# Scaled float16 parts in all three pair passes of an attention and mixture-of-experts kernel

## The chip, the core and the metric

The kernel runs as one program on one core of a Trainium2 chip. The metric is the device time of one execution in microseconds. Three runs of the kernel before took 1152.30, 1151.19 and 1151.82 us; their median, 1151.82 us, is the time that the change is measured against.

## The reference, cut to what matters

```
x   = attention(q, k, v)                 # (4, 8, 768, 64): 3072 tokens of 512
p   = domain_probs / (sum over experts + 1e-9)
out = 0
for e in range(4):
    h    = maximum(x @ w1[e], 0)         # 512 -> 1024
    out += p[:, e] * (h @ w2[e])         # 1024 -> 512
```

Attention is a local window of 16 keys to either side, together with one summary key (a maximum) and one summary value (a mean) of each block of 32 keys, under one softmax. All inputs and outputs are float32, and every expert sees every token, so the matmuls of the four experts are most of the work.

## The kernel before, in words

**Precision.** TensorE is not fed plain float32. A value is split into a high and a low part, and each product is three matmuls: high by high, high by low, low by high. There are two kinds of parts. The wide kind is float32r. The narrow kind is float16; its operands are first multiplied by a power of two taken from the largest absolute value of the operand, and the powers are divided out in the mixing weights (`mixed`, L1006).

**Tokens and passes.** The 3072 tokens are eight blocks of 384 (`TB`). The two blocks of one batch form a pair, and `plan` (L1405) lists six passes: block 0 with experts 0 and 1, block 1 with experts 1 and 0, blocks 0 and 1 with experts 2 and 3, and then pair 1, pair 2 and pair 3 with all four experts each. The first three are the plain passes. A pair pass does its first layer by Strassen's seven products (`SEVEN`, L1157) on halves of tokens, rows and columns: 4 quarters `i` of an expert, 7 products, 6 matmuls of 384 columns each. The second layer of pairs 1 and 2 is plain (`second`, L1083): 6 token tiles, 8 chunks of rows, 3 matmuls of 512 columns. Pair 3 uses seven products there too.

**Which parts where.** `SCALED = NTB // 2 - 2` (L185) is 2: pairs 2 and 3 use float16 parts, the plain passes and pair 1 float32r.

**Weights.** In the plain passes and in pair 1, `weights` (L783) and `w1_operands` (L804) load raw float32 rows and split them with ScalarE (the high part) and GpSimd or VectorE (the low part). `split_weights` (L768) also writes every expert's split w2 to a DRAM tile (`stored`); pair 1 reads it back. For float16, `prepare` (L875) is a generator with 32 jobs, two rows of w1 or w2 each: it loads the rows, makes the scaled parts on ScalarE and VectorE, with the sums for w1 on GpSimd, and writes the parts to DRAM for pair 3. Steps of it are taken at fixed units: `LATE` (11 steps in the last expert of the pass before), and `FIRST` and `SECOND` (10 steps each in every expert's first and second layer). So 4 jobs run ahead of the pass and 28 in it. `fetch_last` (L951) reads the w1 parts back for pair 3.

**Finding the powers.** The largest w1 and w2 values of expert 2 are scanned by VectorE reductions in the plain pass (`scan_plain`, `scan_w2`), those of the other three experts in pair 1 (`scan_w1`, `scan_w2`). `scan_v` (L366) does the same for v of batches 2 and 3, one reduction in each attention piece, and bounds x. `spread_maxima` (L143) then passes a maximum over the partitions by a write to DRAM and a broadcast read, 6 and 8 us of planned matmul time apart.

**Order.** Attention is cut into pieces of 96 queries by 4 heads, 16 in a batch; `ENDS` (L37) says at which piece each pass stops, and `advance` interleaves them with the matmuls in proportion to the work done. Pairs 1 and 2 thus carry pieces of the batches that come next. A piece's probabilities are turned by a DMA transpose (`transposed`, tile awT), and TensorE waits for it before the product with v (tile px). All DMAs are issued in order by one queue, SyncE's. The program is written in priority order, and a scheduler places each engine's instructions after that order and its own estimate of times.

Two buffer pools matter: `x` (14 tiles of 3 KB, for x operands; float32r operands of a pair take all 14, float16 operands 7) and `w2` (8 tiles of 4 KB).

Of the kernel before, what the change touches and what calls it, by code (L numbers as in the profile page):

```python
# [12 lines left out]
I32 = mybir.dt.int32  # L13
# [53 lines left out]
def attn_moe(ctx: ExitStack, tc: tile.TileContext, qvL, qv0, v0L, kD, kT, vT, w1L, w2L, dpL, cst, out):  # L67
# [57 lines left out]
    found = const.tile([P, 20 + 8 + 3 * FC + 4 + 2 + 7 * E], F32, name="found")  # L125
# [17 lines left out]
    def spread_maxima(start):  # L143

        if chain["stage"] == 0:
            if not pending or not start:
# [38 lines left out]
    SCALED = NTB // 2 - 2  # L185
# [180 lines left out]
    def scan_v(n):  # L366
        b, k = n // 16, n % 16
        if not vtop:
            vtop.update(m=facts(4), all=facts(16))
# [79 lines left out]
    def x_operands(pr):  # L449
        if pr >= SCALED:  # L450
            xp = {}
            for w in XS:
                both = sb.tile([P, 2, 2, TB], F16, name=f"x{pr}_{w}", tag="x", bufs=NX)
                xp[w] = both[:, 0], both[:, 1]
        else:
            xp = {w: [x_half(f"x{v}{pr}_{w}") for v in "hl"] for w in XS}

        def split(w, raw, c, lo):
            hi, low = (x[:, :, c : c + QB] for x in xp[w])
            ins = A.copy(hi, raw)  # L460
            if w == "11" and pr < SCALED:
                behind(ins, last_matmul[0])
            lo.tensor_tensor(low, raw, hi if pr >= SCALED else hi.bitcast(F32), op=ALU.subtract)
# [6 lines left out]
        def part(ib, raw):  # L470
            if pr >= SCALED:
                behind(V.tensor_scalar(raw, raw, v_scale[pr][0][:, 0:1], None, op0=ALU.mult), last_matmul[0])
# [293 lines left out]
    stored = {}  # L766

    def split_weights(raw, e, fc, which, lo_engine):  # L768
# [33 lines left out]
    WS = ("11", "s2", "s1", "s3", "12", "s4", "22")  # L802

    def w1_operands(e, pr):  # L804
        ws = {w: w1_part(f"w1{w}{e}_{pr}") for w in WS}
        r1, r2 = (load_weights(w1L, e, 2 * pr + j, "1") for j in range(2))
        a11, a12 = r1[:, 0:256], r1[:, 256:512]
        a21, a22 = r2[:, 0:256], r2[:, 256:512]

        def parts(w, raw, lo):  # L810
            hi, low = ws[w][:, 0:256], ws[w][:, 256:512]
            A.copy(hi, raw)
            lo.tensor_tensor(low, raw, hi.bitcast(F32), op=ALU.subtract)

        parts("11", a11, PL)
        parts("22", a22, V)
        PL.tensor_tensor(a22, a21, a22, op=ALU.add)
        PL.tensor_tensor(a21, a11, a21, op=ALU.subtract)
        PL.tensor_tensor(a11, a22, a11, op=ALU.subtract)
        parts("s2", a11, V)  # L820
        parts("s1", a22, PL)
        parts("s3", a21, V)
        parts("12", a12, PL)
        PL.tensor_tensor(a12, a12, a11, op=ALU.subtract)
        parts("s4", a12, V)
        return ws

    PAIRS = ((1, (3, 1, 0, 2)), (2, (3, 2, 1, 0)), (3, (3, 2, 1, 0)))
    top1 = facts(2 * FC).rearrange("p (w i) -> p w i", i=FC // 2)
    top2, kinds, backs = facts(FC), facts(4), facts(E)  # L830
# [5 lines left out]
    KINDS = ("11", "12", "22", "s3")  # L836

    def scan_w1(ws, i, m):

        if m in SCANS:  # L840
            w = SCANS[m]
            largest(top1[:, KINDS.index(w), i : i + 1], ws[w][:, 0:256].bitcast(F32))

    SCANS = {0: "11", 1: "s3", 2: "12", 3: "22"}

# [3 lines left out]
    top1p = top1.rearrange("p w i -> p (w i)")[:, 0:FC]  # L849

    def scan_plain(fc, w):
        largest(top1p[:, fc : fc + 1], w[0].bitcast(F32))

    def maxima_of(e, plain):

        most = facts(2)
        if plain:
            V.tensor_reduce(most[:, 0:1], top1p, axis=AX.X, op=ALU.max)
        else:
            V.tensor_reduce(kinds, top1, axis=AX.X, op=ALU.max)  # L860
            V.tensor_tensor(kinds[:, 0:1], kinds[:, 0:1], kinds[:, 3:4], op=ALU.add)
            V.tensor_reduce(most[:, 0:1], kinds[:, 0:3], axis=AX.X, op=ALU.max)
        V.tensor_reduce(most[:, 1:2], top2, axis=AX.X, op=ALU.max)
# [9 lines left out]
    half2, PLAIN = {}, (2,)  # L873

    def prepare():  # L875
# [26 lines left out]
        for (which, pr, e, i), after in zip(jobs, jobs[1:] + [None]):  # L902
# [4 lines left out]
            if which == 1:  # L907
                w = sb.tile([P, 2, 2, 512], F16, name=f"w2s{pr}{e}_{i}", tag="w2", bufs=FC)
                wd2[e, i] = room = dram.tile([P, 2, 768], F16, name=f"wd2s{e}_{i}")
                for j, r in enumerate((r1, r2)):  # L910
# [3 lines left out]
                    if j == 0:  # L914
                        keep(room[:, :, 0:256], w[:, 0, :, 0:256])
                    else:
                        keep(room[:, :, 256:768], w[:, 1])
# [33 lines left out]
    def fetch_last(e, i):  # L951

        ws = ready[SCALED + 1, e, i] = {}
        for names in (("11", "12"), ("22",), ("s3", "s1"), ("s2", "s4")):
            t = sb.tile([P, 2, 256 * len(names)], F16, name=f"wl{names[0]}{e}_{i}", tag="w1", bufs=NW1)
            SP.dma_start(t, wd1.pop((e, i, names)))
# [3 lines left out]
    def fetch_whole(e, i):  # L960

        q = sb.tile([P, 2, 768], F16, name=f"wq{e}_{i}", tag="x", bufs=NX)
        SP.dma_start(q, wd2.pop((e, i)))
# [42 lines left out]
    def mixed(pr):  # L1006

        t = pw[:, 2 * pr * (TB // P) : 2 * (pr + 1) * (TB // P), :]
        every = backs.rearrange("p (o e) -> p o e", o=1).broadcast_to([P, 2 * (TB // P), E])
        ins = V.scalar_tensor_tensor(t, t, v_scale[pr][1][:, 0:1], every, op0=ALU.mult, op1=ALU.mult)  # L1010
# [62 lines left out]
    todo = [(PAIRS[0][0], e, i) for e in PAIRS[0][1] for i in range(FC // 2)]  # L1073

    def fetch(until=None):

        while todo and until not in ready:
            key = todo.pop(0)
            ready[key] = w1_operands(*key[1:])
            if until is None:  # L1080
                return
# [10 lines left out]
    def with_fetch(units, pr, e, w2, last):  # L1092
        steps = SECOND if pr and pr >= SCALED else LATE if (pr, e) == (SCALED - 1, PAIRS[0][1][-1]) else ()
        plain = pr is None
        scanned = e in PLAIN if plain else pr == SCALED - 1 and e not in PLAIN
        for n, us in enumerate(units):
            if last and n in (1, 8):
                fetch()
            if scanned:
                if 3 <= n < 3 + FC:  # L1100
                    scan_w2(n - 3, w2[n - 3])
                if n == 3 + FC:
                    maxima_of(e, plain)
# [5 lines left out]
            if (pr, e) == (SCALED, PAIRS[1][1][-1]):  # L1109
                if n in LAST2:  # L1110
                    next(preparing_last, None)
                if n in (12, 15):
                    fetch_last(PAIRS[2][1][0], (n - 12) // 3)
            yield us

    def plain_units(tbs, e, early=0, last=False):
# [24 lines left out]
        for fc in order:  # L1141
            if fc not in w1:
                w1[fc] = weights(w1L, e, fc, "1", PL)
            for tb in tbs:
                us = mm1(fc, tb, w1[fc], KC // 2 if fc < early else 0)
                if e in PLAIN and tb == tbs[0]:
                    scan_plain(fc, w1[fc])
# [4 lines left out]
        yield from with_fetch(second(tbs, e, hT, w2, False), None, e, w2, last)  # L1152
# [119 lines left out]
    def pair_units(pr, e, last=False):  # L1272
# [4 lines left out]
        _, w2 = kept.pop(e, ({}, {}))  # L1277
        kept.clear()
        small = pr >= SCALED
        final = pr == NTB // 2 - 1  # L1280
        hop = {}
        if small and e == dict(PAIRS)[pr][0]:
            mixed(pr)
        for i in range(FC // 2):
            if not small:
                fetch((pr, e, i))
                if i < FC // 2 - 1:
                    fetch((pr, e, i + 1))
            if final:
                at = PAIRS[2][1].index(e) * (FC // 2) + i  # L1290
                for k in range(at, min(at + 3, E * FC // 2)):
                    key = PAIRS[2][1][k // (FC // 2)], k % (FC // 2)
                    if (pr, *key) not in ready:
                        fetch_last(*key)
# [8 lines left out]
            for m, (k, w, x) in enumerate(SEVEN):  # L1303
                first = m < 2
                o = new(k) if first else bank[k]
                both = ready[pr, e, i][w]
                both = both if small else [both[:, v * 256 : (v + 1) * 256] for v in range(2)]
                wh, wl = (v.rearrange("p (c f) -> p c f", f=P) for v in both)
# [31 lines left out]
                if m == 3 and not small:  # L1340
                    for fc in (f1, f2):
                        if fc not in w2:
                            w2[fc] = weights(w2L, e, fc, "2", PL)
                if not small and e not in PLAIN:
                    scan_w1(ready[pr, e, i], i, m)
                passed[0] += 6 * US1
                spread_maxima(small or e == PAIRS[0][1][-1])
                if small and not final and 7 * i + m in FIRST:
                    next(preparing, None)
# [4 lines left out]
        if small:  # L1354
            w2 = {fc: half2.pop((pr, e, fc)) for fc in range(FC)}
        kept[e] = {}, w2
        yield from with_fetch(second(tbs, e, hT, w2, last), pr, e, w2, True)
# [47 lines left out]
    plan = [([0], (0, 1)), ([1], (1, 0)), ([0, 1], (2, 3)), *PAIRS]  # L1405
# [97 lines left out]
```

## Time and profile before

| | us |
|---|---|
| median of three runs | 1151.82 |
| the profiled execution | 1152.57 |
| its span, first to last instruction | 1150.70 |
| TensorE busy | 1110.3 (96%) |
| VectorE busy | 812.3 (71%) |
| ScalarE busy | 667.2 (58%) |
| GpSimd busy | 637.5 (55%) |
| pair 1, from 374.3 to 657.4 of the span | 283.1 |
| pair 2, from 657.4 to 927.8 | 270.4 |
| pair 3 and the end, from 927.8 | 222.9 |

The sum is made against the profiled execution: 1152.57 us, of which 1.87 us lie outside the span. It stands 0.75 us above the median. The passes are told apart by the tiles of TensorE's instructions: the first `pha` with float32r parts starts at 374.5 us, the first with float16 parts at 657.6, and the first that reads pair 3's `wl` at 927.5. Tile names that the rows use: `po` is a second-layer sum, `pha` to `phd` are the seven products' sums, `w,hh` and `w,hl` weights and hidden values in float32r, `w2s` float16 weights of w2, `wss` and `ws` of w1, `found` the room for maxima.

### The profile page before, as it was taken

To read this page: it belongs to the slowest core of one execution; us is meant where nothing else is said; L and a number is where in the kernel's file an instruction comes from. 1 tells how busy PE (TensorE), PEld (TensorE's weight loads), DVE (VectorE), ACT (ScalarE), POOL (GpSimd) and SP (SyncE) were. 2 spreads that over 40 slices of the span, in tenths; PEclk is the share of its full clock that TensorE was granted. 3 is DMA by queue.
4 is the path that set the end of the run, shared out by engine and by line. 5 is a ranking of instruction groups with operands and counts; after the bars stand their busy time and mean duration, and the time that the engine had idled before them with its cause. 6 is when DMAs were issued, how large, how long until landed. Compare 5 with 4: busy or idle time off the path is not lost. (4 is left out here: it accounts for less than half of the span.)

```text
span 1150.7 us, 22284 instructions
## 1 busy us (share of the span) xinstructions
PE 1110.3 (96%) x7620; PEld 862.6 (75%) x7620; DVE 812.3 (71%) x1926; ACT 667.2 (58%) x1827; POOL 637.5 (55%) x770
## 2 busy tenths in 40 slices
PE   9898899999899999999999989999999989999998
PEld 7778789898898988889889755555545458686867
DVE  6669667677677886859866886857856766565653
ACT  5668477675575654637456575756745355445451
POOL 2398588866586764736555555545422547273631
PEclk9999999999899999999999999999999999999999
DMA  6699788986974448377582685868757653535211
GB/s 243 219 273 316 224 244 231 281 198 173 277 216 122 113 123 208 88 216 157 172 247 74 197 247 159 241 151 258 197 167 233 216 185 103 177 97 169 62 32 56
DMA packets 196929, 211.74 MB, mean 184 GB/s; under 512 B 82384, under 2 KB 132816, under 8 KB 196816
## 3 DMA queue, kind: packets, MB, share of 16 engines
q1 hardware_dynamic: 196816, 210.33, 63.6%
q8 instruction: 60, 0.98, 0.3%
q14 instruction: 53, 0.43, 0.2%
HBM read 144.60 MB, written 48.76 MB: 168 GB/s over the span
## 5 line engine op out<-in xcount | busy, mean ns | idle before, releaser
L79 PE MATMUL po<-w,hh 128*128 128x512 f32 x768 | 241.8, 396 | 0.0
L79 PEld LDWEIGHTS po<-w,hh 128*128 128x128 f32 x768 | 141.9, 189 | 30.5
L79 POOL TENSOR_TENSOR ks<-kr,ks 128x304 fp32r<-128x304 f32 x112 | 101.6, 914 | 97.9 <-ACT ks L79 90.9
L79 PE MATMUL po<-w,hl 128*128 128x512 f32 x384 | 152.1, 398 | 0.0
L79 ACT ACTIVATE ms<-ms,nb 96x152 f32<-96x152 f32 x256 | 104.4, 416 | 22.3 <-DVE nb L79 22.0
L79 PE MATMUL po<-w2s,hh 128*128 128x512 f16 x384 | 114.9, 380 | 0.0
L79 PE MATMUL ph<-xh,wh 128*128 128x384 f32 x256 | 88.8, 351 | 10.0 <-ACT wh L79 5.4
L79 DVE TENSOR_TENSOR aw<-ms,aw 96x512 f16<-96x512 f32 x112 | 80.9, 755 | 13.7 <-ACT aw L79 12.8
L79 PE MATMUL ph<-xl,wh 128*128 128x384 f32 x256 | 87.9, 343 | 0.6 <-DVE xl L79 0.6
L79 PE MATMUL ph<-xh,wl 128*128 128x384 f32 x256 | 87.5, 343 | 0.0
L79 ACT CAST aw<-ms 96x512 f16<-96x512 f32 x112 | 53.3, 523 | 55.9 <-issue 36.5
L79 DVE CUSTOM_DVE_ANT_0 ms<-psc,c_sb 96x152 f32<-96x152 f32 x256 | 68.7, 305 | 22.9 <-PE psc L79 21.9
L79 PEld LDWEIGHTS po<-w,hl 128*128 128x128 f32 x384 | 72.3, 188 | 15.9
L79 POOL TENSOR_TENSOR wl<-wr,wh 128x512 fp32r<-128x512 f32 x44 | 60.5, 1378 | 42.5 <-ACT wh L79 41.4
L79 POOL TENSOR_TENSOR qv<-qv,v 128x256 f32<-128x256 f32 x56 | 40.9, 738 | 64.4 <-ACT v L79 63.5
L79 PE MATMUL po<-w2s,hl 128*128 128x512 f16 x192 | 72.8, 379 | 0.0
L79 ACT CAST v<-qv 128x256 bf16<-128x256 f32 x112 | 44.1, 401 | 48.3 <-PE px L79 25.3
L79 ACT CAST ks<-kr 128x304 fp32r<-128x304 f32 x112 | 48.1, 444 | 32.8 <-PE psc L79 20.3
L79 PEld LDWEIGHTS <-hh 128*128 128x128 f16 x384 | 36.2, 98 | 40.9
L79 POOL TENSOR_TENSOR hts<-hts,hr 128x384 f32<-128x384 f32 x16 | 16.0, 1003 | 89.3 <-DVE hts L79 81.5
L79 POOL TENSOR_TENSOR w<-wr,w 128x256 fp32r<-128x256 f32 (+1 forms) x48 | 51.3, 1070 | 23.0 <-ACT w L79 18.1
L79 POOL TENSOR_TENSOR qs<-qv,qs 64x384 fp32r<-64x384 f32 x56 | 60.2, 1076 | 5.7 <-ACT qs L79 1.7
(206 smaller groups left out, 3017.1 us busy)
## 6 DMA issues: line engine op xcount, KB each, us to landing
wr<-in_w1L SPq DMA_DIRECT2D x76, 256.0 KB, 3.6
qv<-in_qvL SPq DMA_DIRECT2D x56, 320.0 KB, 4.3
wd<-w SPq DMA_DIRECT2D x32, 512.0 KB, 4.5
w<-wd SPq DMA_DIRECT2D x32, 512.0 KB, 7.3
kr<-in_kD SPq DMA_DIRECT2D x56, 256.0 KB, 3.6
wr<-in_w2L SPq DMA_DIRECT2D x32, 256.0 KB, 4.7
wr1s<-in_w1L SPq DMA_DIRECT2D x32, 256.0 KB, 3.4
wd1s<-wss SPq DMA_DIRECT2D x32, 256.0 KB, 3.0
```

The costliest lines, as they stand in the source:

```text
L79: ins = getattr(self.engine, name)(*a, **kw)
```

## The change

`SCALED` becomes 1, so that pair 1 too uses float16 parts. `prepare` therefore runs during pair 1 (its first jobs in the last plain expert), writes all of w1's and w2's parts to DRAM, and pairs 2 and 3 read them back: `fetch_parts` (w1, both pairs) and `fetch_second` (w2, pair 2). `w1_operands`, `scan_w1` and the DRAM copies of split w2 for experts 1, 2 and 3 go. The powers of two have to be known earlier: expert 3 is now scanned in the plain pass as expert 2 is, v of batch 1 is scanned too, and for experts 1 and 0 a new generator `look` bounds the largest value by the root of the largest sum of squares. It loads each matrix in 6 parts of 128 x 768 (the last 128 x 256) and lets ScalarE square and sum them; its 24 loads and 24 activations run in pair 1, under the first two experts. The order of the experts in every pair pass is 2, 3, 1, 0. `mixed` is called for each expert instead of once in a pass. Core of the diff:

```diff
-    SCALED = NTB // 2 - 2
+    SCALED = 1
...
-        if which == "2":
+        if which == "2" and e == AGAIN:
             stored[e, fc, "2"] = dram.tile([P, 2, 512], F32, name=f"wd2{e}_{fc}")
             SP.dma_start(stored[e, fc, "2"], w.bitcast(F32))
...
-    def w1_operands(e, pr):
...
-    PAIRS = ((1, (3, 1, 0, 2)), (2, (3, 2, 1, 0)), (3, (3, 2, 1, 0)))
+    PAIRS = ((1, (2, 3, 1, 0)), (2, (2, 3, 1, 0)), (3, (2, 3, 1, 0)))
...
-    def scan_w1(ws, i, m):
...
+    LOOK = 768
+
+    def look(e):
+
+        parts = []
+        for w, top in ((w1L, top1), (w2L, top2)):
+            flat = w[e].rearrange("c p d -> (c p d)").rearrange("(p n) -> p n", p=P)
+            for k, c in enumerate(range(0, FC * DM, LOOK)):
+                parts.append((flat[:, c : min(c + LOOK, FC * DM)], top[:, k : k + 1]))
...
+        for n in range(len(parts) + 2):
+            if n < len(parts):
+                load(parts[n][0])
+            if n >= 2:
+                raw = raws.pop(0)
+                behind(A.activation(raw, raw, AF.Square, accum_out=parts[n - 2][1]), last_matmul[0])
+            yield
+        most = facts(2)
+        V.tensor_reduce(most[:, 0:1], top1[:, 0:sums], axis=AX.X, op=ALU.max)
+        V.tensor_reduce(most[:, 1:2], top2[:, 0:sums], axis=AX.X, op=ALU.max)
...
-    half2, PLAIN = {}, (2,)
+    half2, PLAIN = {}, (2, 3)
...
-                wd2[e, i] = room = dram.tile([P, 2, 768], F16, name=f"wd2s{e}_{i}")
+                wd2[e, i] = room = dram.tile([P, 2, 2, 512], F16, name=f"wd2s{e}_{i}")
...
+    def fetch_second(pr, e, i):
+
+        w = sb.tile([P, 2, 2, 512], F16, name=f"w2l{pr}{e}_{i}", tag="w2", bufs=FC)
+        SP.dma_start(w, wd2[e, i])
+        for j in range(2):
+            half2[pr, e, 2 * i + j] = w[:, j, 0], w[:, j, 1]
...
+            if not plain:
                 passed[0] += us[0]
-                spread_maxima(True)
+                spread_maxima()
+                if pr == SCALED and n % 2:
+                    next(looks.get(e, iter(())), None)
...
+                if m == 5 and pr == PAIRS[1][0]:
+                    fetch_second(pr, e, i)
+                if pr == SCALED:
+                    if (7 * i + m) % 2 == 0:
+                        next(looks.get(e, iter(())), None)
+                    if 7 * i + m in FIRST:
+                        next(preparing, None)
```

## Rows read from the trace of the kernel before

**Rows 1.** Windows: us; busy PE, PEld, DVE, ACT, POOL; clock; DMA; GB/s.

```profile
60.00:130.00 70.00, 66.47 (x486) 57.12 (x485) 53.72 (x128) 50.24 (x154) 56.91 (x59) 0.98 0.99 287
270.00:374.30 104.30, 100.31 (x633) 88.31 (x632) 77.86 (x183) 63.22 (x192) 72.58 (x85) 0.97 0.75 205
374.30:657.40 283.10, 278.77 (x1758) 246.06 (x1756) 215.99 (x560) 159.00 (x476) 163.10 (x212) 0.99 0.60 160
657.40:927.80 270.40, 257.73 (x1684) 140.37 (x1683) 198.38 (x424) 160.13 (x406) 121.90 (x150) 0.99 0.70 209
```

**Rows 2.** TensorE's timeline in pair 1: start us, length us, instruction, how many.

```profile
381.82 0.33 PE L79 MATMUL phc<-xh,w1s 128*128 128x384 f32 x1
383.90 0.33 PE L79 MATMUL pha<-xh,w 128*128 128x384 f32 x1
...
424.41 0.62 PE L79 MATMUL po<-w,hh 128*128 128x512 f32 x2
429.27 0.62 PE L79 MATMUL po<-w,hh 128*128 128x512 f32 x2
```

**Rows 3.** The chain that ended last, in pair 2: start us, us, what, matmuls.

```profile
787.27 7.79 PE po L79 x36
...
801.58 1.95 PE pha L79 x12
```

**Rows 4.** Score matmuls in pair 1 and in pair 2 (groups by form).

```profile
L79 PE MATMUL psc<-ks,qs 128*96 128x152 f32 x120 | 15.3, 249 | 0.0
...
L79 PE MATMUL psc<-ks,qs 128*96 128x152 f32 x96 | 15.6, 282 | 0.0
```

**Rows 5.** Waits of TensorE in pair 2: us in total, times, longest us.

```profile
PE px L79 <- DMA awT<-aw: 4.4, 3, 2.8
PE pha L79 <- ACT x L79: 2.8, 1, 2.8
```

**Rows 6.** Waits of TensorE's weight loads in pair 2, same columns.

```profile
PEld L79 <- DMA wr2t<-in_w2L: 3.1, 1, 3.1
```

**Rows 7.** ScalarE groups in pair 1: busy us, mean ns, then idle before.

```profile
L79 ACT CAST w1s<-wr 128x256 fp32r<-128x256 f32 x56 | 20.2, 405 | 20.5 <-POOL wr L79 20.2
L79 ACT CAST w<-wr 128x256 fp32r<-128x256 f32 x42 | 16.0, 405 | 0.7 <-DVE found L79 0.7
L79 ACT ACTIVATION_READ_ACCUMULATOR ms<-ms,nb 96x1 f32 x60 | 11.4, 191 | 0.0
```

**Rows 8.** ScalarE groups in pair 2 that make scaled parts.

```profile
L79 ACT ACTIVATE w2s<-wr2s,found 128x512 f16<-128x512 f32 x31 | 22.3, 718 | 7.1 <-PE phb L79 3.5 <-DMA wr2s<-in_w2L 2.4 <-PE po L79 1.0
L79 ACT ACTIVATE wss<-wr1s,found 128x512 f16<-128x512 f32 x28 | 19.9, 720 | 15.0 <-POOL wr1s L79 9.9 <-PE po L79 2.6 <-PE phb L79 2.5
L79 ACT ACTIVATE ws<-wr1s,found 128x512 f16<-128x512 f32 x14 | 10.0, 714 | 1.1 <-PE po L79 1.1
L79 ACT ACTIVATE ws<-wr1s,found 128x256 f16<-128x256 f32 x14 | 6.9, 495 | 0.7 <-DMA wr1s<-in_w1L 0.7
```

**Rows 9.** VectorE groups in pair 1: low parts and scans.

```profile
L79 DVE TENSOR_TENSOR w1s<-wr,w1s 128x256 fp32r<-128x256 f32 x42 | 23.2, 562 | 5.4 <-ACT w1s L79 5.2
L79 DVE TENSOR_REDUCE found<-w 128x1 f32<-128x512 f32 x24 | 16.1, 678 | 7.8 <-PE po L79 7.8
L79 DVE TENSOR_REDUCE found<-w 128x1 f32<-128x256 f32 x36 | 14.5, 406 | 0.7 <-PE pha L79 0.7
```

**Rows 10.** VectorE groups in pair 2: low parts of scaled weights.

```profile
L79 DVE SCALAR_TENSOR_TENSOR w2s<-wr2s,found,w2s 128x512 f16<-128x512 f32 x31 | 25.0, 807 | 5.7 <-ACT w2s L79 5.5
L79 DVE SCALAR_TENSOR_TENSOR wss<-wr1s,found,wss 128x512 f16<-128x512 f32 x28 | 21.8, 785 | 6.6 <-ACT wss L79 6.6
```

**Rows 11.** DMA issues on the page: count, KB each, median us to landing.

```profile
w<-wd SPq DMA_DIRECT2D x32, 512.0 KB, 7.3
```

**Rows 12.** Waits of the DMA queue over the span: us, times, longest us.

```profile
SPq L79 <- DVE wss L79: 38.7, 17, 12.9
```

**Rows 13.** ScalarE groups of the first 14 us: the table load.

```profile
L79 ACT ACT_TABLE_LOAD x1 | 1.3, 1283 | 0.7 <-PEq L1493 0.7
```

More of the change, by code (lines that the diff above doesn't have):

```diff
@@ L141, in attn_moe, with spread_maxima @@
     chain = dict(stage=0, due=0.0)
[L143 removed]
+    def spread_maxima():
         if chain["stage"] == 0:
[L146 removed]
+            if not pending:
                 return
@@ L368, in scan_v @@
         if not vtop:
-            vtop.update(m=facts(4), all=facts(16))
+            vtop.update(m=facts(2 * (B - SCALED)), all=facts(16))
         V.tensor_reduce(
@@ L449, in x_operands @@
     def x_operands(pr):
[L450 to L456, printed above, removed]
+        xp = {}
+        for w in XS:
+            both = sb.tile([P, 2, 2, TB], F16, name=f"x{pr}_{w}", tag="x", bufs=NX)
+            xp[w] = both[:, 0], both[:, 1]
         def split(w, raw, c, lo):
             hi, low = (x[:, :, c : c + QB] for x in xp[w])
[L460 to L463, printed above, removed]
+            A.copy(hi, raw)
+            lo.tensor_tensor(low, raw, hi, op=ALU.subtract)
         def fetched(ib):
@@ L1068, in mm2 @@
         yield done, 1.0
[L1073 to L1081, printed above, removed]
+    plan = [([0], (0, 1)), ([1], (1, 0)), ([0, 1], (2, 3)), *PAIRS]
+    looks = {PAIRS[0][1][0]: look(PAIRS[0][1][2]), PAIRS[0][1][1]: look(PAIRS[0][1][3])}
     def second(tbs, e, hT, w2, last):
@@ L1090, in second, with with_steps @@
             yield from mm2(tb, e, range(TB // P), hT, w2)
[L1092 to L1095, printed above, removed]
+    def with_steps(units, pr, e, w2):
+        plain, final = pr is None, pr is not None and e == PAIRS[0][1][-1]
+        if plain:
+            steps = LATE if e == plan[2][1][-1] else ()
+        else:
+            steps = SECOND if pr == SCALED else ()
         for n, us in enumerate(units):
-            if last and n in (1, 8):
-                fetch()
-            if scanned:
+            if plain and e in PLAIN:
                 if 3 <= n < 3 + FC:
@@ L1151, in plain_units @@
         kept[e] = {fc: w1[fc] for fc in order[-4:]}, w2
-        yield from with_fetch(second(tbs, e, hT, w2, False), None, e, w2, last)
+        yield from with_steps(second(tbs, e, hT, w2, False), None, e, w2)
     SEVEN = (
@@ L1305, in pair_units @@
                 o = new(k) if first else bank[k]
-                both = ready[pr, e, i][w]
-                both = both if small else [both[:, v * 256 : (v + 1) * 256] for v in range(2)]
-                wh, wl = (v.rearrange("p (c f) -> p c f", f=P) for v in both)
+                wh, wl = (v.rearrange("p (c f) -> p c f", f=P) for v in ready[pr, e, i][w])
                 xh, xl = xp[x]
@@ L1353, in pair_units @@
             return
[L1354 to L1357, printed above, removed]
+        w2 = {fc: half2.pop((pr, e, fc)) for fc in range(FC)}
+        yield from with_steps(second(tbs, e, hT, w2, last), pr, e, w2)
     steps = []
@@ L1421, in attn_moe @@
             else:
-                units, ahead = ahead or plain_units(tbs, e, last=n == 2 and e == experts[-1]), None
+                units, ahead = ahead or plain_units(tbs, e), None
             for us, pace in units:
```

137 lines of the change are left out of this document (52 added, 85 removed).

## Prediction

> **What bounds the kernel now.** I read the windows view first, by pass [rows 1]. TensorE is busy 278.77 of 283.10 us in pair 1 and 257.73 of 270.40 us in pair 2. No other engine passes 77% in either (VectorE in pair 1, 215.99 of 283.10), and the DMA engines stand at 0.60 and 0.70. So the rate of the matmuls bounds both passes. The same rows show that pair 1, whose layers have the same shapes as pair 2's, takes 12.7 us longer although it waits less: 4.33 us without a matmul against 12.67. The timeline says why. With float32r parts, twelve first-layer matmuls start in 383.90 - 381.82 = 2.08 us, 173 ns each, and 21 second-layer matmuls between 424.41 and 429.27, 231 ns each [rows 2]. With float16 parts the chain shows twelve in 1.95 us, 162.5 ns each, and 36 in 7.79 us, 216.4 ns each [rows 3]. The granted clock is 0.99 in both passes [rows 1], the 2.4 GHz level for nearly all of them, so the difference belongs to the parts.
>
> **Term 1, the matmuls of pair 1.** The code gives 4 experts x 4 quarters x 7 products x 6 = 672 matmuls of 384 columns, and 4 experts x 6 token tiles x 8 chunks x 3 = 576 of 512. In float32r they take 672 x 0.1733 + 576 x 0.2314 = 249.8 us; in float16 672 x 0.1625 + 576 x 0.2164 = 233.8 us. The change takes out **16.0 us** on the engine that bounds the pass. The counts stay, and so does pair 2's rate.
>
> **Term 2, what is left beside the matmuls.** Pair 1: 283.1 - 249.8 = 33.3 us, of which 4.3 are idle and 29.0 belong to attention. By `ENDS` pair 1 holds 15 pieces. Pair 2 has 15 by plan as well, but the scheduler has placed only 12 of them in its window (96 score matmuls at 8 to the piece, against 120 in pair 1 [rows 4]): 270.4 - 233.8 - 12.7 = 23.9 us. That is 1.93 and 1.99 us to a piece, so idle time and attention separate well, and attention's part is kept. What moves is idle time.
>
> **Term 3, idle time in pair 1.** It is 4.3 us now. The work of making scaled parts moves into the pass, 28 of 32 jobs of it, where 4 ran before; what pair 1 did for itself goes.
> - ScalarE loses 20.2 + 16.0 = 36.2 us of splits [rows 7]. It gains 24 more jobs of the 28 that cost 22.3 + 19.9 + 10.0 + 6.9 = 59.1 us in pair 2 [rows 8], so 50.7 us. The trace shows no squares. By the slope between 512 and 256 columns (0.714 and 0.495 us [rows 8]) one of 768 takes 0.93 us, and the sum is read out in 0.19 [rows 7]: 20 x 0.93 + 4 x 0.495 + 24 x 0.19 = 25.2 us, all under the first two experts. In the pass ScalarE goes from 159 to about 199 us of 278, 71%; under the first two experts it is near 80%.
> - VectorE loses 23.2 + 16.1 + 14.5 us [rows 9] and two smaller groups, and gains 24/28 of 25.0 + 21.8 us [rows 10] and of two smaller groups: it stays near 216 us, of 278 77%. GpSimd gets less.
> - DMA. Now 160 GB/s x 283.1 us = 45.3 MB [rows 1]. Out go 24 reads of 512 KB (12.6 MB, [rows 11]), 6.3 MB of w1, 4.0 MB of early jobs. In come 14.7 MB of rows, 20.1 MB of parts to DRAM, 8.4 MB for the looks and 1.8 MB for pair 2: 67.4 MB in about 270 us, 250 GB/s. The stretch from 60 to 130 us ran at 287 GB/s with the engines 0.99 busy [rows 1]. So pair 1 comes near the limit that this stretch shows, and over its first half, with the looks, to it.
>
> The nearest rows for such a pass are pair 2, with the same jobs, and the 60 to 130 stretch, with the DMA full. Pair 2's 12.67 us scaled from 12 to 15 pieces is 15.8; the full stretch's 3.53 of 70 us is 13.5 over 268. Bounds: 4.3, if the covers hold as now, and 28, if the first half idles at twice pair 2's rate. I take **15.8**, since pair 2 has the same work on the same engines: 11.5 us lost.
>
> By the Trainium skill, DMA: Bandwidth & Descriptors, under Where 436 GB/s comes from, transfers between HBM and SBUF are bound at about 358 GB/s. By that 250 GB/s would leave a third free, and an estimate from it would put pair 1's idle time nearer the lower bound; the row at 287 GB/s and 0.99 is below it, and I go by the row, since this kernel's transposes share the same engines.
>
> **Term 4, idle time in pair 2.** `prepare` leaves: 59.1 us of ScalarE [rows 8], 46.8 us of VectorE [rows 10] and two smaller groups, 33.8 MB. In come 12.8 MB of w1 parts and 8.4 MB of w2 parts: 56.5 MB fall to 44, 166 GB/s. The waits that the trace names here are 4.4 us on transposed probabilities, 2.8 us at the end for pair 3's x [rows 5], and 3.1 us of weight loads for the last w2 sums [rows 6]. The last two are not of `prepare` and stay; the transposes come back in part. Bounds 1 and 12.7; I take **5**, 7.7 us gained. The reads are issued a quarter of an expert or more ahead; were that lead gone, one would cost its landing, 7.3 us for 512 KB [rows 11].
>
> **Term 5, the plain passes.** 24 writes of the same size as those reads [rows 11] go from stretches where DMA is 0.75 to 0.99 busy [rows 1]. Scanning expert 3 adds 16 VectorE reductions of 0.678 us, and v of batch 1 adds 16 of about 0.41 (nearest group, 406 ns [rows 9]): 17 us. From 270 us VectorE is busy 77.9 of 104.3 us, so there is cover; TensorE waits 4.0 us there [rows 1]. Those 4.0 us are the most that can be gained in this stretch; I bound the term by -5, a little more for the stretches before it, and by +4, the same wait once more. I take **-1**, near the middle, since writes go and scans come. `mixed` by expert is 16 small VectorE operations instead of 2, behind a matmul each, with nothing waiting but the sums of the second layer; the chains that pass maxima around lie beside matmuls as they do now. Both at nothing; without that cover, some 0.3 us each time.
>
> **Sum.** -16.0 + 11.5 - 7.7 - 1 = -13.2. From 1152.57 that is 1139.4 us; the profiled execution stands 0.75 above the median, so **1139 us**, 1.1% below 1151.82.
>
> **Rivals.**
> *A, the forecast*, 1139; its own range, with pair 1's idle time between 10 and 20 us, is 1133 to 1144.
> *B, the jobs are free where they land.* Pair 1 idled only 4.3 us with splits, scans and reads of its own, and VectorE's load stays. If the looks and stores hide, its idle time is 8, pair 2's 3, and the plain passes give 3: -16.0 - 6 - 3 = -25, 1127. For it: TensorE's named waits in pair 2 were mostly not on scaled parts [rows 5, 6]. Against it: the DMA load of term 3.
> *C, the DMA queue is late.* All transfers go through one queue in order, and pair 1 gets some 84 more of them: 24 jobs bring about 108, the looks 24, 48 leave. A store to DRAM waits for VectorE's low part (38.7 us in 17 waits, the longest 12.9 [rows 12]); behind it stand loads of attention and transposes. TensorE then waits for transposed probabilities in every piece; in pair 2 the longest such wait was 2.8 us [rows 5]. At 2 us to each of 15 pieces, with the 8.3 us of pair 2's idle time that are not such waits, pair 1 idles 38.3 us: -16.0 + 34.0 - 7.7 - 1 = +9, 1161. It decides from 1.4 us to a piece (33.2 us of idle time in both passes, less 5 for pair 2, plus 1 for the plain passes, less 8.3, over 15). For it: the sum of bytes. Against it: TensorE lost only 3.5 us in 70 at a full DMA [rows 1].
> *D, ScalarE has to change its table for each square.* ScalarE mixes exponentials, relu and copies with one table load of 1.283 us in all [rows 13]. If the square stood in another set, 24 squares with a load before and after take 61.6 us of ScalarE under two experts. One such expert needs about 43 us of it for attention, first layer and jobs, 12.6 for looks and 31 for loads: 87 us against some 66 of the pass, so 1139 + 2 x 21 = 1181. The Trainium skill, ScalarE: Activation LUTs, under Table sets, lists cheap functions that every set carries and does not name the square among them; that one load serves three functions here agrees with the rest of its rule. Three functions already share one load in this trace, so I give the case little.
> That the change does not do what it says can be put aside: the parts' type follows from `SCALED` alone.
>
> **How the numbers follow.** A 0.52, B 0.25, C 0.19, D 0.04. What a measurement of this kernel can tell from no change is about 0.2%, 2.3 us. A and B are faster; C spreads around its point and gives 0.04 to no change and 0.15 to slower; D is slower. Faster 0.77, same 0.04, slower 0.19. The range takes in A, nearly all of B and half of C: 1126 to 1158.
>
> **What would show it.** In the changed profile the first layer of pair 1 should run at 162 ns and the second at 216 ns a matmul; pair 1 should last near 278 us with 16 idle, pair 2 near 263 with 5. ScalarE should be near 199 us in pair 1, and `ACT_TABLE_LOAD` still one. Landing times of transposes in pair 1 well above those of the page before, and waits of px on awT in most pieces, would show C. It is wrong if pair 1 is not shorter than before, or if time appears in the plain passes, where I see room for a few us only.

## The result, and the profile after

The changed kernel took 1137.84 us in the median of four runs (1136.07 to 1143.18), the kernel before 1152.06 beside it: a ratio of 0.9876, interval 0.9834 to 0.9919. That is faster, and 1139 had been forecast. In a later series, beside other variants, the same kernel gave 1140.26 us against 1149.72, a ratio of 0.9917 (0.9889 to 0.9944). The profiled execution took 1136.07 us, its span 1134.2.

First the windows view of the changed kernel. The rows answer to [rows 1], pass by pass: two stretches of the plain passes, pair 1, pair 2, and pair 3 with the end.

```profile
60.00:130.00 70.00, 67.57 (x484) 58.09 (x484) 52.87 (x134) 50.66 (x155) 57.35 (x58) 0.95 0.83 227
270.00:377.20 107.20, 103.24 (x650) 90.86 (x649) 85.79 (x215) 62.50 (x184) 65.11 (x76) 0.97 0.68 189
377.20:653.50 276.30, 264.13 (x1758) 144.58 (x1757) 221.50 (x526) 194.32 (x520) 135.52 (x172) 0.99 0.89 268
653.50:911.50 258.00, 254.33 (x1683) 139.24 (x1682) 136.86 (x333) 109.35 (x315) 65.55 (x91) 1.00 0.54 146
911.50:1134.20 222.70, 219.34 (x1678) 164.07 (x1677) 133.89 (x254) 105.69 (x228) 101.96 (x116) 1.00 0.34 105
```

Pair 1 went from 283.1 to 276.3 us, pair 2 from 270.4 to 258.0. Pair 3 stayed (222.7 and 222.9). The plain passes got longer, 377.2 us instead of 374.3. In pair 1 TensorE's busy time fell by 14.6 us and its idle time rose from 4.3 to 276.30 - 264.13 = 12.2; in pair 2 the idle time fell from 12.7 to 3.7.

Why the busy time fell stands in TensorE's timeline inside pair 1 of the changed kernel (start us, length us, instruction, how many). It answers to [rows 2]:

```profile
419.75 0.38 PE L79 MATMUL po<-w2s,hl 128*128 128x512 f16 x1
419.97 0.59 PE L79 MATMUL po<-w2s,hh 128*128 128x512 f16 x2
...
421.70 1.14 PE L79 MATMUL phb<-x_t,ws 128*128 128x384 f16 x6
422.67 0.38 PE L79 MATMUL po<-w2s,hl 128*128 128x512 f16 x1
```

Nine second-layer matmuls start in 421.70 - 419.75 = 1.95 us, 217 ns each, and six first-layer ones in 0.97 us, 162 ns each: the rates of pair 2 before [rows 3].

Where the idle time of pair 1 lies is seen when the pass is cut more finely (windows of the changed kernel, same columns; the first two rows overlap with the third):

```profile
377.20:380.70 3.50, 0.31 (x2) 0.10 (x1) 1.93 (x5) 1.88 (x6) 1.61 (x3) 0.99 1.08 213
380.70:387.50 6.80, 6.24 (x36) 3.35 (x36) 6.80 (x17) 4.60 (x15) 4.03 (x6) 0.50 0.97 339
...
377.20:407.50 30.30, 24.71 (x172) 14.13 (x170) 27.95 (x67) 24.83 (x69) 18.83 (x24) 0.89 1.04 307
407.50:515.40 107.90, 105.33 (x693) 57.22 (x693) 82.81 (x208) 81.11 (x217) 53.15 (x64) 1.00 0.84 256
515.40:653.50 138.10, 134.10 (x895) 73.23 (x894) 110.72 (x252) 88.38 (x236) 63.53 (x84) 1.00 0.90 268
```

Of the 12.2 us, 5.6 fall into the first 30, where VectorE is busy 92% and the DMA engines are full. The rest of the looks' half gives 2.6, the second half 4.0. So nearly half of it lies at the entry of the pass: TensorE stands still until 380.7, and for the 6.8 us after that its granted clock is at the half level, 1.2 GHz (0.50). The kernel before has no idle time at all in its first 30 us of pair 1. The timeline around the entry, all engines, says on what TensorE waits first:

```profile
371.62 0.33 SPq L79 DMA_DIRECT2D xr<-xd  x1
...
373.61 0.32 SPq L79 DMA_DIRECT2D xr<-xd  x1
...
376.83 0.62 DVE L79 TENSOR_SCALAR xr<-xr,found 128x768 f32<-128x768 f32 x1 [0.95 <-DMA xr<-xd]
...
379.65 0.62 DVE L79 TENSOR_SCALAR xr<-xr,found 128x768 f32<-128x768 f32 x1 [1.54 <-POOL x L79]
...
380.71 0.48 PE L79 MATMUL pha<-x,ws 128*128 128x384 f16 x1 [3.19 <-ACT x L79]
```

The last two quarters of raw x (tile xr) are requested at 371.6 and 373.6 us, because two buffers (`chunk`) serve all of them in turn; the DMA queue has a wait of 1.4 us for VectorE's xr in this stretch. The last one landed 5.9 us after its request, at 379.5, just when GpSimd's part of x, which the row names, ended too. Its scaling runs at 379.65, and the first product of the pass starts a microsecond behind it. The waits of TensorE in pair 1 confirm that there is no second wait of that size, and none on transposed probabilities (us in total, times, longest us):

```profile
PE phb L79 <- ACT phb L79: 3.4, 3, 1.3
PE pha L79 <- ACT x L79: 3.2, 1, 3.2
PE phb L79 <- DVE phc L79: 1.7, 2, 1.0
```

In pair 2 TensorE's waits for transposes [rows 5] have gone. What is left is pair 3's x, and in the view of the weight loads the wait of [rows 6], 2.6 us where it was 3.1:

```profile
PE pha L79 <- ACT x L79: 2.3, 1, 2.3
PE px L79 <- ACT p L79: 1.1, 1, 1.1
```

```profile
PEld L79 <- DMA wr2t<-in_w2L: 2.6, 1, 2.6
```

**The plain passes.** They run the same 2504 matmuls in both kernels. One window over all of them, in the kernel before and then in the changed one:

```profile
0.00:374.30 374.30, 354.37 (x2504) 312.08 (x2505) 265.20 (x694) 242.39 (x718) 250.42 (x294) 0.98 0.81 232
```

```profile
0.00:377.20 377.20, 357.23 (x2504) 313.29 (x2504) 269.94 (x734) 238.44 (x700) 240.33 (x280) 0.97 0.73 204
```

Idle time is 19.9 and 20.0 us. The 2.9 us are busy time, and the granted clock is a hundredth lower. So the added scans cost TensorE no wait in these two profiles; its matmuls ran for longer at the half level, 20.5 us where the kernel before has 13.7.

### The profile page after: what moved, and what is told of

Read it like the earlier page. It is cut to its first block, busy times and chain, and to the rows that moved or that the text cites. A ratio compares the mean times of both kernels' runs of the same rounds, so it can differ in the third digit from the quotient of the medians.

```text
span 1134.2 us, 21978 instructions
## 1 busy us (share of the span) xinstructions
PE 1095.0 (97%) x7620; PEld 761.2 (67%) x7620; DVE 762.2 (67%) x1845; ACT 647.8 (57%) x1763; POOL 543.4 (48%) x658
## 5 line engine op out<-in xcount | busy, mean ns | idle before, releaser
L79 PEld LDWEIGHTS <-hh 128*128 128x128 f16 x768 | 72.1, 98 | 81.0
L79 PE MATMUL po<-w,hh 128*128 128x512 f32 x384 | 122.5, 400 | 0.0
L79 PE MATMUL po<-w2l,hh 128*128 128x512 f16 x384 | 114.9, 379 | 0.0
L79 PEld LDWEIGHTS <-wls 128*128 128x128 f16 x768 | 74.2, 98 | 47.8
L79 PEld LDWEIGHTS po<-w,hh 128*128 128x128 f32 x384 | 72.2, 192 | 15.6
L79 PEld LDWEIGHTS <-wl 128*128 128x128 f16 x576 | 55.8, 98 | 39.6 <-DMA wr2t<-in_w2L 2.6
L79 PE MATMUL pha<-x,wl 128*128 128x384 f16 x384 | 74.0, 326 | 2.8 <-ACT x L79 2.3
L79 PE MATMUL po<-w,hl 128*128 128x512 f32 x192 | 76.3, 401 | 0.0
L79 PE MATMUL phb<-x_t,wls 128*128 128x384 f16 x384 | 72.9, 326 | 0.0
L79 PE MATMUL po<-w2l,hl 128*128 128x512 f16 x192 | 72.8, 379 | 0.0
```

Source lines behind the costliest of these rows:

```text
L79: ins = getattr(self.engine, name)(*a, **kw)
```

## The experiments

Before the runs the theories were these. The forecast's own: pair 1's idle time comes from the looks and jobs that now load ScalarE, VectorE and the DMA there. Against it: the late x at the entry is what costs. And for the plain passes: the scans of expert 3 made them longer. All kernels differ from the changed one by the edit shown, and each ratio is to the runs of the kernel before beside it. A single time has a spread of some us, so one profile of each kernel is also cut in three: **plain**, to the end of the last second-layer matmul of the plain passes; **pair 1**, from there to the first product of pair 2; **rest**, from plain's end to the end of the span. "Entry" is the wait of pair 1's first product, "idle" the time without a matmul in pair 1.

| kernel | median us | ratio to before (interval) | plain | entry | pair 1 | idle | rest |
|---|---|---|---|---|---|---|---|
| before | 1152.06 | 1 | 374.7 | 0 | 282.9 | 4.3 | 776.0 |
| changed | 1137.84 | 0.9876 (0.9834 to 0.9919) | 377.5 | 3.2 | 276.0 | 12.2 | 756.7 |
| changed, again | 1140.26 | 0.9917 (0.9889 to 0.9944) | 380.0 | 3.7 | 276.8 | 13.4 | 758.9 |
| no looks | 1134.81 | 0.9874 (0.9835 to 0.9913) | 379.4 | 1.7 | 274.9 | 12.4 | 758.6 |
| looks twice | 1151.63 | 1.0012 (0.9988 to 1.0035) | 376.6 | 4.7 | 287.9 | 23.8 | 768.9 |
| loads twice | 1143.09 | 0.9942 (0.9920 to 0.9964) | 375.8 | 4.3 | 284.9 | 19.7 | 765.6 |
| squares twice | 1149.90 | 0.9978 (0.9950 to 1.0006) | 380.8 | 3.4 | 288.0 | 20.6 | 768.8 |
| expert 3 unscanned | 1138.36 | 0.9888 (0.9847 to 0.9929) | 383.3 | 2.0 | 277.0 | 13.2 | 758.9 |
| x early | 1134.11 | 0.9868 (0.9829 to 0.9906) | 377.5 | 0 | 276.8 | 14.2 | 754.9 |
| x early, on VectorE | 1130.53 | 0.9819 (0.9790 to 0.9849) | 374.0 | 0 | 274.7 | 13.0 | 752.3 |
| same, looks late | 1135.80 | 0.9854 (0.9818 to 0.9890) | 379.9 | 0 | 277.0 | 13.8 | 754.7 |
| same, looks at thirds | 1133.48 | 0.9849 (0.9823 to 0.9876) | 377.5 | 0 | 274.7 | 11.7 | 752.3 |
| same, no looks | 1130.37 | 0.9836 (0.9799 to 0.9872) | 375.8 | 0 | 273.2 | 10.5 | 751.0 |
| on VectorE alone | 1145.89 | 0.9959 (0.9938 to 0.9981) | 377.7 | 10.4 | 283.4 | 20.7 | 765.7 |

**No looks.** Loads and squares are replaced by constants.

```diff
-        for n in range(len(parts) + 2):
...
-            yield
+        for k in range(2):
+            for n in range(sums):
+                V.memset(parts[k * sums + n][1], 0.25)
+        yield
```

> Left out: the 24 loads and 24 squares of the looks; the largest sums of squares of experts 1 and 0 are set to a constant, the rest of the chain stays. Theory E (entry): the 12.2 us of idle time in pair 1 come mostly from its entry, where the x operands are late, and the looks cost TensorE next to nothing: 0 to 2 us faster than the changed kernel, 1136 to 1139 us, and the wait of the first pha for x stays at 2 to 4 us. Theory L (load): the looks, with 8.4 MB and 23.6 us of ScalarE under the first two experts, are why the first half of pair 1 idles 8.2 us against 4.0 in the second: 4 to 8 us faster, 1130 to 1134 us, with the idle time of the two halves alike.

Pair 1 is 1 to 2 us shorter, the rest of the program takes as long as in the changed kernel (758.6 us beside 756.7 and 758.9), and the two ratios are the same. Pair 1 idles as long as with the looks, 12.4 us; what it is shorter by is the clock, 3.4 us at the half level instead of 6.8. The looks are all but hidden, though they make up an eighth of ScalarE's work in the pass.

**Looks twice, loads twice, squares twice.** Three edits of `look`: each part loaded and squared twice; only the load doubled; only ScalarE's work doubled, by a copy with a sum ahead of each square.

```diff
                 load(parts[n][0])
+                load(parts[n][0])
...
+                raws.pop(0)
```

```diff
+                behind(A.activation(raw, raw, AF.Copy, accum_out=parts[n - 2][1]), last_matmul[0])
                 behind(A.activation(raw, raw, AF.Square, accum_out=parts[n - 2][1]), last_matmul[0])
```

> Every look loads and squares each part twice: 8.4 MB and some 24 us of ScalarE more, all in the first half of pair 1. Theory E: transfers and squares lie beside the matmuls, 0 to 3 us slower, 1138 to 1141 us. Theory L: the first half would need 267 + 61 = 328 GB/s where the fullest stretch of the kernel before moved 287, and ScalarE would be busy 130 of 138 us: 8 us slower or more, 1146 or above, with DMA share at 0.95 or over and waits of px on awT in many pieces.

> Of the doubled looks only the loads: each part is loaded twice and squared once, 8.4 MB more in the first half of pair 1, ScalarE as in the changed kernel. Doubling both cost 13.8 us. Theory D (DMA limit): the first half of pair 1 has the DMA full (0.88 at 267 GB/s, 1.00 at 306 with the looks doubled), and loads and transposes come late; nearly all of the 13.8 us are here: 1147 to 1152 us. Theory S (ScalarE): the squares stand in ScalarE's order ahead of the evictions that TensorE waits for; loads alone cost little: 1138 to 1141 us.

> Of the doubled looks only ScalarE's part: each part is loaded once, and one more activation of the same shape (a copy with a sum) stands before each square, some 24 us of ScalarE more in the first half of pair 1. Theory D: 0 to 3 us slower than the changed kernel, 1138 to 1141 us. Theory S: most of the 13.8 us, 1146 us or above, with longer waits of phb and pha for ScalarE.

Pair 1 grows by 11.5, 8.5 and 11.6 us over the mean of the two profiles of the changed kernel (276.4). The costs are neither additive nor the reverse of taking the looks out. For the loads alone both theories missed: 1143.09 us lies between them. Windows over the first half of pair 1, in the order changed kernel, no looks, both, loads, squares:

```profile
377.20:515.40 138.20, 130.03 (x864) 71.35 (x863) 110.77 (x274) 105.94 (x284) 71.99 (x88) 0.98 0.88 267
```

```profile
379.40:516.85 137.45, 129.12 (x867) 70.95 (x867) 109.34 (x267) 91.83 (x241) 72.03 (x88) 0.99 0.74 218
```

```profile
376.60:520.55 143.95, 128.62 (x867) 70.89 (x866) 107.83 (x264) 121.89 (x331) 70.83 (x87) 0.98 1.00 306
```

```profile
375.80:518.25 142.45, 129.59 (x860) 70.58 (x860) 109.20 (x268) 106.57 (x284) 77.03 (x88) 0.98 1.01 306
```

```profile
380.80:524.80 144.00, 128.19 (x845) 70.73 (x845) 110.84 (x261) 121.43 (x331) 69.72 (x87) 0.95 0.83 247
```

TensorE idles 8.2, 8.3, 15.3, 12.9 and 15.8 us in these halves. With the loads doubled the DMA engines are full (1.01) and ScalarE is where it was; with the squares doubled the DMA is at 0.83 and ScalarE at 84%. Either alone is enough to add idle time, 4.7 and 7.6 us in this half. Part of what the doubled squares cost is the clock: pair 1 has 17.1 us at the half level there, 6.8 in the changed kernel. So load on these engines can cost TensorE what the forecast says, but the looks as they stand don't: at a DMA share of 0.88 and ScalarE at 77% of the half, they still fit into gaps.

**Expert 3 unscanned.** The reductions over expert 3 in the plain passes go, and constants take the place of its maxima.

```diff
-                if 3 <= n < 3 + FC:
+                if 3 <= n < 3 + FC and e == 2:
...
-                    if tb == tbs[0]:
+                    if tb == tbs[0] and e == 2:
```

> Left out: the 16 reductions that scan expert 3 in the plain pass (its maxima are set to a constant). Theory E: they take 10.8 us of VectorE where the x operands are made, so x comes earlier and 1 to 4 us are gained, 1134 to 1137 us, part of it in the plain pass, which grew by 2.9 us, part at the entry. Theory L: no change beyond 1 us, and the plain pass's 2.9 us are a lower clock at 68 us and its spread.

The ratio is about the changed kernel's, and the plain passes took 383.3 us in this profile, longer and not shorter. One profile says little of a few us, since the plain passes lie between 374.0 and 380.8 us in the twelve profiles that keep the scans; but nothing here supports that the scans lengthened them.

**x early.** The raw quarters of x get tiles of their own in the pool `x`, and the planned lead of the x parts is changed in all passes. The two were not tried apart.

```diff
-            raw = sb.tile([P, 4, 2, QB], F32, name=f"xr{pr}_{ib}", tag="chunk", bufs=CHUNKS)
+            raw = sb.tile([P, 4, 2, QB], F32, name=f"xr{pr}_{ib}", **(dict(tag="x", bufs=NX) if pr == SCALED else dict(tag="chunk", bufs=CHUNKS)))
...
-    XLEAD, XGAP, LAST = 6.0, 4.5, 0.4
+    XLEAD, XGAP, LAST = 2.0, 3.0, 0.4
```

> The raw x of pair 1 is loaded into buffers of the x pool, which has room there, so that the third and fourth part no longer wait for the first two, and the parts are planned 2 and 3 us apart instead of 6 and 4.5 (in all passes). Theory E: the first pha of pair 1 no longer waits 3.2 us, and the 8 us that the entry loses between the last plain matmul and 20 us later shrink to 2 to 4: 1131 to 1135 us. Theory L: the load is unchanged, so the time is the changed kernel's within 2 us, and the entry idles for something else.

The entry wait is gone, but pair 1 is no shorter (276.8 us) and idles 14.2 us. The timeline of GpSimd and of TensorE in this kernel shows what came in its place:

```profile
372.31 8.34 POOL L79 TENSOR_TENSOR ks<-kr,ks 128x304 fp32r<-128x304 f32 x1
...
385.34 1.76 PE L79 MATMUL phd<-x_t,wss 128*128 128x384 f16 x5 [6.67 <-POOL x_t L79]
```

A subtraction that takes 0.9 us on average took 8.34, the low parts of x stood behind it on GpSimd, and TensorE waited 6.7 us for one of them. So the next edit takes those parts from GpSimd:

```diff
-            lo.tensor_tensor(low, raw, hi, op=ALU.subtract)
+            (V if pr == SCALED else lo).tensor_tensor(low, raw, hi, op=ALU.subtract)
```

> As e3_x_early, and pair 1's low parts of x are all made on VectorE, none on GpSimd. In e3 one GpSimd subtraction at 372 us took 8.34 us while VectorE ran without a gap, and the x behind it came late (phd waited 6.7 us). Theory E: the entry is held by the making of x; with GpSimd out of its chain neither the first pha nor phd waits more than 1.5 us, the entry loses 2 to 4 us instead of 8, and the time is 1128 to 1132 us. Rival: VectorE's 16 more subtractions, 5.4 us, come at the same place and take back what GpSimd gave: 1133 to 1136 us, with waits of pha or phd on DVE x.

With both edits neither wait is there, the rest falls to 752.3 us, and the ratio of 0.9819 is the lowest of all: this version beats the kernel before by 1.8% and the changed one by about 0.6%, though its interval overlaps that of the changed kernel's first series. Windows of pair 1 and pair 2:

```profile
374.00:648.70 274.70, 261.68 (x1757) 143.96 (x1755) 220.59 (x531) 192.36 (x515) 130.25 (x164) 0.99 0.89 265
648.70:902.60 253.90, 252.84 (x1678) 138.58 (x1676) 136.34 (x333) 108.71 (x317) 66.15 (x92) 1.00 0.55 147
```

But pair 1 idles 274.70 - 261.68 = 13.0 us, no less than the 12.2 and 13.4 of the changed kernel. The window of its first 30 us, and TensorE's longest waits in pair 1 by name, show where the time went:

```profile
374.00:404.00 30.00, 24.13 (x177) 14.34 (x175) 27.17 (x71) 24.96 (x65) 13.64 (x16) 0.94 0.96 296
```

```profile
PE phb L79 <- ACT phb L79: 5.3, 4, 1.8
PE pha L79 <- DVE nb L79: 2.7, 3, 1.9
```

The entry still idles 5.9 us, where a loss of 2 to 4 was forecast, in shorter waits for VectorE and ScalarE, with VectorE busy 91% there and the DMA engines at 0.96. So the late x was where TensorE stood, but taking it away gave back no idle time, and Theory E, that the entry is held by the making of x, is not borne out although its time came true. What this version gains over the changed kernel's profile in the rest, 4.4 us, is 1.3 in pair 1, where half-level time falls from 6.8 to 3.4 us, 2.4 in pair 2, and 0.7 in pair 3. Measured from its first product to pair 3's, pair 2 falls from 257.3 to 254.9 us: the wait of 2.3 us for pair 3's x, which the same lead serves, is gone. (The window above ends 1.0 us before pair 3's first product, that of the changed kernel 0.7 us behind it.)

**Looks late, at thirds, and out, with x early on VectorE.** Three variants of that kernel: looks begin only at step 8 of each expert's first layer; they are taken at every third step instead of every second; they are replaced by constants as in the first experiment.

```diff
-                    if (7 * i + m) % 2 == 0:
+                    if (7 * i + m) % 2 == 0 and 7 * i + m > 7:
```

> As e7_x_on_dve, and the looks of each of the two experts start 8 units later, so that their loads don't stand ahead of the scaled weights' loads at the entry (in e3 ScalarE waited 8.15 us for w1 rows there). Theory D: the entry is where the DMA queue is fullest, so 1 to 3 us less than e7, 1126 to 1131 us, and first landings of w1 rows after the entry near 4 us instead of 6.7. Rival: the same bytes come 8 us later and cost the same: equal to e7 within 1 us.

> As e7_x_on_dve, and in the first layers a step of a look comes every third unit instead of every second, so that the squares are spread over more of an expert. Theory S (squares cost where ScalarE is dense; one more activation each cost 12 us, removing them gained 3): 0 to 3 us faster than e7's 1130.5, 1127 to 1131 us, with ScalarE's share of the first 30 us of pair 1 below e7's 24.96 of 30. Rival (the looks are free as they stand): equal to e7 within 1.5 us, 1129 to 1132.

> As e7_x_on_dve, with the looks' loads and squares left out as in e1 (constants in their place). It bounds what any better place for the looks can gain once the entry is mended. Theory S: 3 to 6 us below e7, 1125 to 1128 us, as TensorE's idle time in the first half of pair 1 falls from e7's 8.6 us to 5 or less. Theory E (the entry alone matters, looks hide): within 2 us of e7, 1129 to 1132 us.

Where the looks stand makes no gain: the rest is 754.7 and 752.3 us, and both medians lie above 1130.53, where the forecasts had them below or equal. Without any looks the rest is 751.0. The 1.3 us are less than the 2.2 by which the two profiles of the changed kernel differ, and the medians (1130.53 and 1130.37) do not tell the two kernels apart. With the looks and the entry wait both gone, pair 1 still idles 10.5 us. What no run takes out are the 28 jobs that make scaled parts; that they bring this idle time, as the forecast had it, is left standing but not shown.

**The changed kernel once more, and VectorE alone.** In the second only the low parts are moved, without the buffers and the lead.

> The changed kernel once more, unaltered, on the chip and beside the runs of the other three. The plain passes ended at 377.5 us in the changed kernel's profile and between 374.0 and 383.3 in eight variants that leave those passes as they are for the first 340 us. Theory N (spread): here too they end between 374 and 384 us, the clock's half-rate stretches before 377 us decide where, and the 2.9 us by which they grew are no cost of the change; the time is 1135 to 1141 us. Rival (the scans and new steps cost it): the plain passes end at 377 us or later, with VectorE named in waits that the kernel before does not have.

> The changed kernel with one edit: pair 1's low parts of x are made on VectorE instead of GpSimd; buffers and planned distances stay. It divides e7's 7.3 us. Theory G (GpSimd, held off while VectorE runs without a gap, is what delays x): 3 to 7 us faster than the changed kernel, 1131 to 1135 us. Rival (the two buffers that raw x waits for are): the first pha still waits 2 us or more for x and the gain is under 2 us, 1136 to 1139 us.

The unaltered kernel shows the entry wait again (3.7 us). The second was to test whether GpSimd alone was what made x late: the wait became 10.4 us, and the kernel slower than the changed one (0.9959). Its timeline at the entry, then its windows there:

```profile
371.12 0.33 SPq L79 DMA_DIRECT2D w3d<-found  x1
...
375.52 0.33 SPq L79 DMA_DIRECT2D w3e<-w3d  x1
376.27 0.60 SPq L79 DMA_DIRECT2D xr<-xd  x1
377.60 1.55 SPq L79 DMA_DIRECT2D xr<-xd  x1
384.02 0.62 DVE L79 TENSOR_SCALAR xr<-xr,found 128x768 f32<-128x768 f32 x1 [8.03 <-DMA xr<-xd]
...
388.12 0.48 PE L79 MATMUL pha<-x,ws 128*128 128x384 f16 x1 [10.38 <-ACT x L79]
```

```profile
380.00:393.70 13.70, 4.72 (x17) 2.67 (x17) 9.68 (x29) 5.94 (x19) 1.47 (x1) 0.50 1.03 379
393.70:407.70 14.00, 12.74 (x117) 7.64 (x115) 13.64 (x36) 11.44 (x33) 10.69 (x12) 1.00 0.63 174
```

The last raw quarters are requested 4 to 5 us later than in the changed kernel, and land behind other loads, 7.7 and 8.3 us after the request instead of 5.2 and 5.9. The buffers are not what held the request here: the queue waited 3.0 us for the write of a maximum (w3d), whose broadcast read (w3e) now stands ahead of the raw quarters; in the changed kernel it stands behind them. So this edit moved x's place in the queue as well, and the run doesn't settle whether GpSimd made x late. It shows what a late request costs. With the requests early, as in the two versions before, making the low parts on VectorE took away the wait of 6.7 us.

**The clock.** Every execution also records its mean granted clock. Over the 53 executions of the kernel before that ran beside these experiments the mean is 0.9916 (0.985 to 0.996), over the ten of the changed kernel 0.9857 (0.981 to 0.991). Twice the missing share, times the span, is the time at the half level: 19.4 and 32.5 us. Half of that is lost, an estimate that takes every such stretch as bound by TensorE, so the changed kernel pays 6.6 us more for its clock. Taking half of that time off each execution leaves medians of 1140.8 us before and 1122.5 and 1123.4 after: 17 to 18 us of gain, of which some 11 arrive. The same count gives 24.8 us at the half level for the version with x early on VectorE, and 37 to 39 for looks twice, squares twice and VectorE alone. Loads twice, with an entry wait of 4.3 us, has 31.7, like the changed kernel.

## Why the prediction was right, step by step

**Term 1 was right.** The rates of 162 and 217 ns appeared, and busy time in pair 1 fell by 14.6 us where 16.0 was the sum. The clock explains the remainder: pair 1 has 6.8 us at the half level after the change and had 3.4 before, which is 1.7 us lost. This is the largest term of the sum, and it came as argued.

**Term 2 held.** Pair 1 without its matmuls and its idle time is 276.3 - 233.8 - 12.2 = 30.3 us (29.0 before), of which 1.7 is again the clock. In pair 2 it is 258.0 - 233.8 - 3.7 = 20.5 (23.9 before); 1.7 us of that difference is a half-level stretch that only the kernel before has there, the other 1.7 were not traced further.

**Term 3 was right in sign, a little large, and wrong about the place.** Idle time in pair 1 became 12.2 us, not 15.8. The loads came near the forecast: ScalarE 194 us (199 forecast), VectorE 221.5 (216), DMA 268 GB/s (250). But the looks, put "all under the first two experts" with ScalarE "near 80%", are not a cause: at that load they still hide, as the runs without them show, and doubling them shows where they stop to hide. Nearly half of the idle time lies at the entry, which the prediction did not name: it followed the x operands as a wait of pair 2 [rows 5] and did not ask who makes them for pair 1, now that the first jobs, the scans and the looks stand in the same stretch. Yet mending the late x left the idle time as it was. So the ground of the 15.8, the same jobs on the same engines as in pair 2, is neither shown nor refuted; that it came within 3.6 us is partly luck. The upper bound of 28 doesn't come out of its own words: pair 2's rate in one half and twice it in the other make 1.5 x 15.8 = 23.7.

The squares came out at 0.85 us where 0.93 had been worked out, by the groups of ScalarE in pair 1:

```profile
L79 ACT ACTIVATE lk<-lk 128x768 f32<-128x768 f32 x20 | 17.0, 850 | 0.0
...
L79 ACT ACTIVATION_READ_ACCUMULATOR lk<-lk 128x1 f32 x24 | 4.9, 206 | 0.0
...
L79 ACT ACTIVATE lk<-lk 128x256 f32<-128x256 f32 x4 | 1.7, 415 | 0.0
```

Together 23.6 us, 25.2 forecast.

**Term 4 was right.** Pair 2 idles 3.7 us (5 forecast), at 146 GB/s (166). The two waits that were to stay, pair 3's x and the last weight loads, stayed, at 2.3 and 2.6 us.

**Term 5 came out with the other sign.** The plain passes took 2.9 us more, where 1 less was the sum and 4 more the bound. In the twelve profiles of kernels that keep the scans they take 374.0 to 380.8 us, 377.7 in the mean, against 374.7 in the one profile of the kernel before, so the size is not sharp. The bound's reason, a longer wait, did not come; the clock did, which no term had: the plain passes spend 20.5 to 27.3 us at the half level in every profile after the change and 13.7 before. Its price over the whole program is the 6.6 us above. Which part of the change lowers it was not found: the run without scans of expert 3 has nearly the same clock (0.987 in the mean of its four). This stays open.

So the time came out close because errors offset each other, and that is luck. From profile to profile pair 1 and pair 2 gained 2.3 and 4.7 us more than forecast, and the plain passes lost 3.9 us against it; over many executions the forecast of 13.2 us stands against 17 to 18 us of gain with the clock taken out, less 6.6 us of clock.

**The rivals.** *B*, the jobs are free, was half right: the looks do hide, but pair 1 idled 12.2 us, not 8, and the clock cost its share, so the time stayed above 1127. Jobs and stores were never taken out. *C*, the late DMA queue, did not come. Its sign would have been longer landings and waits of px on transposes, of which pair 1 has none; the DMA issues of the changed kernel in pair 1, and the waits of its DMA queue over the span, show

```profile
awT<-aw SPq DMA_TRANSPOSE x16, 4.4
```

```profile
SPq L79 <- DVE wss L79: 23.0, 18, 2.6
```

a landing of 4.4 us for a transpose, where the kernel before had 4.2 in pair 1, and a longest wait for a low part of 2.6 us, where [rows 12] had 12.9. *D*, a table load for each square, did not come either: among ScalarE's groups of the changed kernel, over its whole span, there is one load.

```profile
L79 ACT ACT_TABLE_LOAD x1 | 1.3, 1283 | 0.7 <-PEq L1472 0.7
```

## What to carry to other kernels

When work is moved into a pass, look at its entry: the operands that the first matmul needs compete with the first jobs, for the helper engines and for a place in the DMA queue. But a wait that is named there is not yet the cause of the idle time: here it was taken away and other waits of the same stretch took its place, so count the idle time after the mending, and not the wait. A helper engine at 77% could still hide an eighth of its work while nothing more was added, so a share says little about the price; doubling and removing the work says it. And a gain on the bounding engine is to be counted against the clock of many executions, not of one profile.

## What the runs showed of the hardware that was not expected

**A GpSimd subtraction of 0.9 us took 8.34** with x early, while VectorE ran without a gap from 369 to 385 us, most of it operations on two operands. GpSimd spans are rough, but TensorE's wait of 6.7 us for what stood behind it is not. The Trainium skill, GPSIMD Engine Reference, under Specifications, says that GpSimd shares its SBUF interfaces with VectorE, with contention from VectorE instructions that have two SBUF inputs. The row agrees with that, but no run here takes this cause alone.

**Time at the half level is not simply the price of a wait.** After a wait of 3.2 us at the entry TensorE ran 6.8 us at the half level, and with the wait of 10.4 us the clock was at 0.50 for 13.7 us from 380.0, 2.3 us after TensorE had stopped, 5.6 of them behind the wait. But waits of 4.7 and 4.3 us (looks twice, loads twice) came with only 3.4 us at the half level, and the four kernels with x early on VectorE, whose first product does not wait, have 3.4 us as well, between 387 and 394 us. So the longest wait came with the longest stretch, but the price of one wait can't be read from these runs.
